# Hash attention and two dense layers: weight loads six slots later, a move two slots later, warm products without a buffer, PSUM halves exchanged

## The chip, the cores and the metric

One core of one Trainium2 chip. The metric is the device time of one execution in microseconds. TensorE (PE) multiplies matrices into PSUM, which has eight banks; VectorE (DVE), ScalarE (ACT) and GpSimd (POOL) do the rest; SyncE (SP) issues nearly all DMAs. Each engine works through its own instructions in order, so an instruction that waits holds up all that stand behind it on its engine. That holds for SP as well: a DMA whose wait is not over keeps the later DMAs from being issued.

## The reference

Attention over 2 batches, 8 heads, 768 positions of width 64, then two dense layers on 1536 tokens of width 512 with an inner width of 2048.

```
q_bits = (q @ proj > 0);  k_bits = (k @ proj > 0)      # 6 bits each
mask   = bucket(q_bits)[:, None] == bucket(k_bits)[None, :]
scores = where(mask, q @ k.T / sqrt(64), -1e9)
attn   = exp(scores - max) / (sum + 1e-9)
x      = attn @ v, heads side by side                  # 1536 x 512
h = x @ w_in;  g = h * tanh(softplus(h));  x = g @ w_out
h = x @ w_in2; g = P(h) / (Q(h) + 1e-6);   out = g @ w_out2
```

P is a cubic and Q a quadratic in h. The weights come as 64-bit numbers and are turned into fp32 pairs (a rounded high part and the rest), and every large product is done as three products of such parts.

## The kernel before, in words

**Attention.** The 16 heads run one behind the other in a software pipeline of *slots*, six to a head: slot 6h + c computes the scores of chunk c of head h (`st`) and, for the head after it, the products from which the row maxima come (`smax`). A table `order` gives every step its first slot, and within a slot the steps go out in the table's order. In the last slot of a head come the value products (`pv`, L307, 24 matmuls), the sums (`dsum`, L431), and for every second head `vsum`. So the PE alternates: six score slots, then a value block.

**What a head needs beforehand.** Head h needs in SBUF: `qB` (rounded q, with the codes of q in rows 0 to 31 and the negated row maxima in row 31), `qX` (the rest of q, in whose first 64 rows a copy of the rounded half belongs) and `KK`. The maxima of head h come from `smax(h, 0..5)`, are gathered on VectorE by `fin_a` (tile `stt`) in slot 6h - 1, and `fin_b` writes them into row 31 of `qB` with four small DMAs, two issued by SP and two by GpSimd. The first score product of head h (L406) waits for these. `move_k` and `move_x` copy parts of k into `KK`; `move_h(h)` (L265) copies 64 rows of `qB` into `qX`, over rows that `move_x(h)` (L261) reads.

**Buffers w0, w1, w2.** The raw input of head h (`load`, L219, slot 6h - 24) lies in buffer w0, w1 or w2, by h modulo 3. Its last readers are `lo(h)` on VectorE (L70, tile qX) and `codes(h)` on the PE, in slot 6h - 7. After the last heads the three buffers take weight chunks 0, 1 and 2 of the first dense layer: `first(f, n)` (L552) loads quarter n of chunk f from a scratch copy in DRAM, in slots FIRST[f] + 2n, from SP. With the values before, chunk 1 starts in slot 66, chunk 2 in slot 72 and chunk 0 in slot 78. The last users of the buffers are head 13 (w1, slot 71), head 14 (w2, slot 77) and head 15 (w0, slot 83).

**Ring.** `weights` converts weight chunks beside the heads: every six slots one ring load (L119), three VectorE operations (L100 to L106), a split on GpSimd, and for chunks 0 to 2 two stores to the scratch copy (L138, L139).

**After a head.** `evac` and `devac` (ScalarE, L447 and L456) read the value block's PSUM tile; `gather`, `recip`, `store` and `spread` bring the reciprocal sums back through SP's DMAs.

**PSUM.** In attention all tiles come from a pool of four buffers of two banks each (`two_banks`). In the opening, `warm(n)` issues n small products of ones whose result nobody reads; they had a tile of their own. After attention the dense stage opens two pools of four banks: `hp` for the first product of a layer (L686), `yp` for the second (L704, L706). The pool that is opened first gets the lower four banks. A dense tile waits for the readers of the attention tile that held its banks.

**Dense stage.** Step i multiplies chunk f of block t (12 matmuls into an h tile), ScalarE and VectorE turn it into g (L729, L730, L70), and 12 matmuls add into four y tiles. Beside the first steps VectorE converts the remaining weight chunks.

Of the kernel before, what the change touches and what calls it, by code (L numbers as in the profile page):

```python
# [9 lines left out]
F32 = mybir.dt.float32  # L10
# [6 lines left out]
PSUM = bass.MemoryType.PSUM  # L17
# [8 lines left out]
NC = S // 128  # L26
BIG = 2.0 ** 40
NBITS = 6
EARLY, SHARED, FIRST = 7, 3, (78, 66, 72, 60, 60, 60, 60)
W_AT, W_LEAD = 5, 4  # L30
POOL_LO = (("lo", 1), ("lo", 2))
ENG = dict(
    lo="dd", hi="aa", xhi="a", xlo="dd", whi="pppp", wlo="pppp",
# [11 lines left out]
def attention_moe_moe(ctx: ExitStack, tc: tile.TileContext, kq, v, proj2, cst, eye, w1, w2, ab, out):  # L45
    nc = tc.nc

    def pool(stack, name, bufs=1, **kw):
        return stack.enter_context(tc.tile_pool(name=name, bufs=bufs, **kw))
# [120 lines left out]
    def attention(actx, tctx):  # L170
# [9 lines left out]
        ring[0] = pool(actx, "ring0", RING[0])  # L180
        ps = pool(actx, "ps", 4, space=PSUM)

        def two_banks(name):
            return ps.tile([128, 2, 512], F32, tag="s", name=name)

        p_raw = ac.tile([128, 64], F32, tag="pr", name="pr")
        cs_t = ac.tile([32, 4], F32, tag="cst", name="cst")
# [8 lines left out]
        ones = v_p.tile([128, 32], F32, tag="ones", name="ones")  # L196
        wones = v_p.tile([128, 128], F32, tag="wones", name="wones")
# [126 lines left out]
        def codes(h):  # L324
            if not 0 <= h < B * H:
                return
            p = [two_banks("cp") for _ in range(1 + (h == 0))]
            ct[h] = p[0][:, 0], p[-1][:, 1]
            code_products(h)


        warm_up = []

        def warm(n):
            if not warm_up:
                warm_up.append(two_banks("wm")[:, 0])
            for _ in range(n):
                nc.tensor.matmul(out=warm_up[0][0:32, 0:128], lhsT=ones, rhs=wones, start=True, stop=True)  # L338

        def code_k(h, of=(0, 1)):  # L340
            if not 0 <= h < B * H:
# [24 lines left out]
        def smax(h, c):  # L366
            if not 0 <= h < B * H:
                return
            if c == 0:
                mt[h] = sm_p.tile([128, NC], F32, tag="m", name="m")  # L370
            p = two_banks("mp")
            for a in range(2):
                nc.tensor.matmul(  # L373
                    out=p[:, a, 0:HALF], lhsT=qB[h % 4][:, c * 128:(c + 1) * 128], rhs=qhalf(KK[h % 4][:, 0], a),
                    start=True, stop=True,
                )
            nc.vector.tensor_reduce(out=mt[h][:, c:c + 1], in_=halves(p), op=ALU.max, axis=AX.XY)  # L377
# [167 lines left out]
        def first(f, n):  # L545
# [26 lines left out]
            ("lo", lo, -7, 1),  # L572
            ("code_q", code_q, -7, 1),
            ("move_x", move_x, -7, 1),
            ("move_h", move_h, -7, 1),
            ("recip", recip, 11, 1),
            ("store", store, 11, 1),
            ("norm", norm, 23, 0),
# [6 lines left out]
            ("gather", gather, 6, 1),  # L585
            ("spread", spread, 12, 1),
            ("vred", vred, -6, 0),
            ("load", load, -24, 1),
            ("load_v", load_v, -10, 0),
            ("first", first, FIRST, -2),  # L590
# [29 lines left out]
        def coef():  # L620
            nc.scalar.activation(out=babs, in_=ab_t[:, 4:6], func=ACT.Abs)

        start = (
            ("get", 0), ("load", 0), ("get", 1), ("load", 1), ("load", 2), ("warm", 5), ("khi", 0), ("qhi",), ("codes", 0),
            ("khi", 2), ("klo",), ("warm", 4), ("signs", 0), ("qlo",), ("hi", 1), ("khi", 1), ("get", 2), ("move_x", 0),
            ("smax", 0, 0), ("warm", 1), ("move_k", 1), ("lo", 1), ("smax", 0, 1), ("warm", 1), ("hi", 2), ("lo", 2),
            ("move_h", 0), ("load", 3), ("smax", 0, 2), ("warm", 1), ("move_x", 1), ("smax", 0, 3), ("warm", 1),
            ("smax", 0, 4), ("warm", 1), ("smax", 0, 5), ("codes", 1), ("fin_a", 0), ("fin_b", 0), ("code_k", 1),
            ("code_q", 1), ("move_k", 2), ("load_v", 0), ("move_h", 1), ("warm", 4),
            ("warm", 4), ("st", 0, 0), ("smax", 1, 0), ("coef",),  # L630
        )

        def run():
            memsets()
            fns = {o[0]: o[1] for o in order}
            fns.update(get=get, coef=coef, khi=khi, qhi=qhi, qlo=qlo, klo=klo, signs=signs)
            done.update((name, (0,)) for name in ("hi", "lo", "move_k", "code_k", "code_q"))
            for name, *k in start:
                if name == "warm":
                    warm(*k)  # L640
                    continue
                done.add((name, tuple(k)))
                fns[name](*k, **({"fn": lo_pool} if (name, *k) in POOL_LO else {}))
            for g in range(last):
                slot_ops(g)
# [7 lines left out]
    def moe(mctx, tctx, tail):  # L653
        by_tile = dict(reuse_waits="tile")
        w2pool = pool(mctx, "w2", **by_tile)
        ring[1] = pool(mctx, "ring1", RING[1], **by_tile)
        g_p = pool(mctx, "g", GB, **by_tile)
        t_p = pool(mctx, "t", 2, **by_tile)
        hp = pool(mctx, "hp", 4, space=PSUM, **by_tile)
        yp = pool(mctx, "yp", 4, space=PSUM, **by_tile)  # L660
        late = []

        def wp(f):
# [214 lines left out]
    with tc.manual_schedule():  # L878
        nc.scalar.preload_act_table_set("natural_log_exp_and_others")
        tctx = ExitStack()  # L880
        with ExitStack() as actx:
            run, tail = attention(actx, tctx)
            run()
        with ExitStack() as mctx:
            run = moe(mctx, tctx, tail)
            run()
# [55 lines left out]
```

## Time and profile before

| | us |
|---|---|
| median of 3 runs | 787.3 (786.08 to 787.31) |
| the profiled execution | 787.76 |
| its span (first to last instruction) | 786.0 |
| PE busy | 763.2 |
| VectorE busy | 588.0 |
| ScalarE busy | 420.9 |
| GpSimd busy | 73.3 |

Attention ends at about 256 us of the span, the first dense layer at about 520. In the profile a group of instructions is named by its line, engine and tiles (`sp<-qB,kk` is a product of qB and kk into the tile sp). Busy shares come in 40 slices of 19.65 us each; PEclk is the clock granted to the PE, in tenths of full speed. An idle time in brackets is the engine's idle time before the instruction, with what ended it.

### The profile page before, as it was taken

To read this page: it belongs to the slowest core of one execution; us is meant where nothing else is said; L and a number is where in the kernel's file an instruction comes from. 1 tells how busy PE (TensorE), PEld (TensorE's weight loads), DVE (VectorE), ACT (ScalarE), POOL (GpSimd) and SP (SyncE) were. 2 spreads that over 40 slices of the span, in tenths; PEclk is the share of its full clock that TensorE was granted. 3 is DMA by queue.
4 is the path that set the end of the run, shared out by engine and by line. 5 is a ranking of instruction groups with operands and counts; after the bars stand their busy time and mean duration, and the time that the engine had idled before them with its cause. 6 is when DMAs were issued, how large, how long until landed. Compare 5 with 4: busy or idle time off the path is not lost.

```text
span 786.0 us, 11698 instructions
## 1 busy us (share of the span) xinstructions
PE 763.2 (97%) x4172; PEld 600.6 (76%) x4172; DVE 588.0 (75%) x1084; ACT 420.9 (54%) x684; POOL 73.3 (9%) x103
## 2 busy tenths in 40 slices
PE   9999999997789999999999999999999999999998
PEld 4767767675566788888888888887888888888886
DVE  5687888885563689855646677659998988888886
ACT  3556656564345444332121333468886766777764
POOL 6323223331210000000000000000000000000000
PEclk9999999999889999999999999999999999999999
DMA  4765764655541434425544588420000100010001
GB/s 132 186 191 162 221 188 110 189 144 137 145 121 34 150 126 148 148 67 168 172 147 161 168 259 267 159 80 1 1 1 1 54 0 1 1 44 11 1 0 55
DMA packets 56650, 85.50 MB, mean 109 GB/s; under 512 B 20112, under 2 KB 28304, under 8 KB 56592
## 3 DMA queue, kind: packets, MB, share of 16 engines
q1 hardware_dynamic: 55424, 84.69, 36.1%
q8 instruction: 33, 0.54, 0.3%
q14 instruction: 25, 0.20, 0.1%
q0 software_dynamic: 1024, 0.03, 0.1%
q10 hardware_dynamic: 144, 0.03, 0.0%
HBM read 57.71 MB, written 14.73 MB: 92 GB/s over the span
## 4 chain that ended last, share of the span: by engine, by line
PE 88%; DVE 5%; DMA 3%; ACT 2%; SPq 1%; issue 1%; DVEq 0%; ACTq 0%
PE h L686 30%; PE y L706 17%; PE y L704 14%; PE sp L406 9%; PE pv L307 6%; PE mp L373 5%; PE pv L431 3%; DMA qB<-stt 2%; PE cp L319 1%; PE wm L338 1%; DVE w L70 1%; DVE t L103 1%; SPq L552 1%; DVE r L106 1%; DMA r<-w 1%
## 5 line engine op out<-in xcount | busy, mean ns | idle before, releaser
L686 PE MATMUL h<-xh,w 128*128 128x512 f32 x768 | 205.0, 389 | 1.6 <-ACT dv L456 1.6
L686 PEld LDWEIGHTS h<-xh,w 128*128 128x128 f32 x768 | 144.2, 188 | 32.0 <-ACT dv L456 2.0
L377 DVE TENSOR_REDUCE m<-mp 128x1 f32<-128x768 f32 x96 | 91.9, 958 | 39.6 <-PE mp L373 35.1
L70 DVE TENSOR_TENSOR gl<-ep,gh 128x512 fp32r<-128x512 f32 x96 | 65.9, 686 | 71.0 <-ACT ep L730 70.0
L729 ACT ACTIVATE gh<-h 128x512 fp32r<-128x512 f32 x48 | 28.7, 599 | 151.1 <-PE h L686 137.9
L686 PE MATMUL h<-xl,w 128*128 128x512 f32 x384 | 102.6, 389 | 0.0
L706 PE MATMUL y<-w,gh 128*128 128x512 f32 x384 | 96.3, 389 | 0.0
L704 PE MATMUL y<-gh,w 128*128 128x512 f32 x384 | 94.8, 389 | 0.0
L411 ACT ACTIVATE e<-sp 128x768 f32<-128x768 f32 x96 | 76.1, 814 | 26.8 <-PE sp L406 25.1
L706 PEld LDWEIGHTS y<-w,gh 128*128 128x128 f32 x384 | 72.1, 188 | 14.9
L686 PEld LDWEIGHTS h<-xl,w 128*128 128x128 f32 x384 | 72.1, 188 | 15.0
L704 PEld LDWEIGHTS y<-gh,w 128*128 128x128 f32 x384 | 72.1, 188 | 15.0
L406 PE MATMUL sp<-qB,kk 128*128 128x384 f32 x192 | 53.9, 363 | 15.0 <-DMA qB<-stt 14.7
L307 PE MATMUL pv<-e,vf 128*64 128x384 f32 x384 | 64.7, 487 | 0.0
L736 ACT ACTIVATE ep<-h 128x512 f32<-128x512 f32 x48 | 28.6, 595 | 52.1 <-PE h L686 52.1
L106 DVE SCALAR_TENSOR_TENSOR r<-r,t 128x256 int32<-128x256 int32 (+1 forms) x114 | 52.1, 457 | 4.7
L103 DVE SCALAR_TENSOR_TENSOR t<-r,t 128x256 int32<-128x256 int32 (+1 forms) x114 | 52.2, 458 | 3.9
L373 PE MATMUL mp<-kk,qB 128*128 128x384 f32 x192 | 53.9, 364 | 0.0
L706 PE MATMUL y<-w,gl 128*128 128x512 f32 x192 | 53.3, 392 | 0.5 <-DVE gl L70 0.4
L307 PEld LDWEIGHTS pv<-e,vf 128*64 128x64 f32 x384 | 27.4, 137 | 34.1 <-issue 33.8
L738 DVE TENSOR_TENSOR n<-n,ep 128x512 f32<-128x512 f32 x48 | 33.1, 690 | 26.9 <-ACT n L737 26.9
L704 PE MATMUL y<-gl,w 128*128 128x512 f32 x192 | 51.4, 390 | 0.1
(79 smaller groups left out, 1038.3 us busy)
## 6 DMA issues: line engine op xcount, KB each, us to landing
r<-w SPq DMA_DIRECT2D x100, 256.0 KB
w<-r SPq DMA_DIRECT2D x64, 128.0 KB
w<-w SPq DMA_DIRECT2D x16, 512.0 KB
r<-w SPq DMA_DIRECT2D x14, 512.0 KB
kq<-kq SPq DMA_DIRECT2D x16, 384.0 KB
kk<-qB SPq DMA_DIRECT2D x15, 384.0 KB
kk<-qX SPq DMA_DIRECT2D x16, 192.0 KB
qX<-qB SPq DMA_DIRECT2D x16, 192.0 KB
```

The lines of the kernel that those rows point to most:

```text
L70: nc.vector.tensor_tensor(out=o, in0=i, in1=f32(h), op=ALU.subtract)
L103: lambda: nc.vector.scalar_tensor_tensor(out=t, in0=r[:, :, 1], scalar=-0x40000000, in1=t, op0=ALU.bitwise_and, op1=ALU.bitwise_or),
L106: lambda: nc.vector.scalar_tensor_tensor(out=o, in0=r[:, :, 0], scalar=29, in1=t, op0=ALU.logical_shift_right, op1=ALU.bitwise_or),
L307: nc.tensor.matmul(out=o[64 * a:64 * a + 64, 0:HALF], lhsT=w, rhs=qhalf(x, a), start=start, stop=stop)
L373: nc.tensor.matmul(out=p[:, a, 0:HALF], lhsT=qB[h % 4][:, c * 128:(c + 1) * 128], rhs=qhalf(KK[h % 4][:, 0], a), start=True, stop=True,)
L377: nc.vector.tensor_reduce(out=mt[h][:, c:c + 1], in_=halves(p), op=ALU.max, axis=AX.XY)
L406: nc.tensor.matmul(out=p[:, a, 0:HALF], lhsT=kk[:, c * 128:(c + 1) * 128], rhs=qq[:, a * HALF:(a + 1) * HALF], start=(i == 0), stop=(i == 1),)
L411: nc.scalar.activation(out=wide(e), in_=halves(p), func=ACT.Exp, scale=1.0 / D ** 0.5)
L686: nc.tensor.matmul(out=p, lhsT=w[:, c * 128:(c + 1) * 128], rhs=x[:, c, :], start=(n == 0), stop=(n == 11))
L704: nc.tensor.matmul(out=y[m], lhsT=w[:, DM + m * 128:DM + (m + 1) * 128], rhs=g, **s)
L706: nc.tensor.matmul(out=y[m], lhsT=g[:, m * 128:(m + 1) * 128], rhs=w[:, DM:2 * DM], **s)
L738: nc.vector.tensor_tensor(out=v_, in0=v_, in1=u, op=ALU.mult)
```

## The change

`FIRST` moves the loads of chunks 0, 1 and 2 six slots later each (84, 72, 78 in place of 78, 66, 72). `move_h` goes from slot 6h - 7 to slot 6h - 5, and in the table from behind `move_x` to behind `vred`. `warm` takes the tile that the next call of `two_banks` will return and writes into that, where it had one of its own; the single warm products after `smax(0, 0)` and `smax(0, 1)` are gone. `yp` is opened before `hp`.

```diff
-EARLY, SHARED, FIRST = 7, 3, (78, 66, 72, 60, 60, 60, 60)
+EARLY, SHARED, FIRST = 7, 3, (84, 72, 78, 60, 60, 60, 60)
...
+        ahead = []
+
         def two_banks(name):
-            return ps.tile([128, 2, 512], F32, tag="s", name=name)
+            return ahead.pop() if ahead else ps.tile([128, 2, 512], F32, tag="s", name=name)
...
-        warm_up = []
-
         def warm(n):
-            if not warm_up:
-                warm_up.append(two_banks("wm")[:, 0])
+            if not ahead:
+                ahead.append(two_banks("wm"))
             for _ in range(n):
-                nc.tensor.matmul(out=warm_up[0][0:32, 0:128], lhsT=ones, rhs=wones, start=True, stop=True)
+                nc.tensor.matmul(out=ahead[0][0:32, 0, 0:128], lhsT=ones, rhs=wones, start=True, stop=True)
...
             ("move_x", move_x, -7, 1),
-            ("move_h", move_h, -7, 1),
             ("recip", recip, 11, 1),
...
             ("vred", vred, -6, 0),
+            ("move_h", move_h, -5, 1),
             ("load", load, -24, 1),
...
-            ("smax", 0, 0), ("warm", 1), ("move_k", 1), ("lo", 1), ("smax", 0, 1), ("warm", 1), ("hi", 2), ("lo", 2),
+            ("smax", 0, 0), ("move_k", 1), ("lo", 1), ("smax", 0, 1), ("hi", 2), ("lo", 2),
...
+        yp = pool(mctx, "yp", 4, space=PSUM, **by_tile)
         hp = pool(mctx, "hp", 4, space=PSUM, **by_tile)
-        yp = pool(mctx, "yp", 4, space=PSUM, **by_tile)
```

## Rows read from the trace of the kernel before

**Rows 1.** The page: busy share of the PE, and its granted clock in 40 slices.

```profile
PE 763.2 (97%) x4172; PEld 600.6 (76%) x4172; DVE 588.0 (75%) x1084; ACT 420.9 (54%) x684; POOL 73.3 (9%) x103
...
PEclk9999999999889999999999999999999999999999
```

**Rows 2.** The PE's waits: line, what it waited for, us in total, times, longest.

```profile
PE sp L406 <- DMA qB<-stt: 14.7, 3, 5.8
PE h L686 <- ACT dv L456: 1.6, 1, 1.6
```

**Rows 3.** Timeline (start us, us, instruction): value products of heads 9 to 14.

```profile
151.96 4.04 PE L307 MATMUL pv<-e,vf 128*64 128x384 f32 x24
...
165.93 4.04 PE L307 MATMUL pv<-e,vf 128*64 128x384 f32 x24
...
179.47 4.04 PE L307 MATMUL pv<-e,vf 128*64 128x384 f32 x24
...
199.80 4.04 PE L307 MATMUL pv<-e,vf 128*64 128x384 f32 x24
...
220.27 4.04 PE L307 MATMUL pv<-e,vf 128*64 128x384 f32 x24
...
239.32 4.09 PE L307 MATMUL pv<-e,vf 128*64 128x384 f32 x24
```

**Rows 4.** Timeline from 180 to 192 us: the first of the three waits.

```profile
180.08 0.21 DVE L386 STREAM_TRANSPOSE stt<-smt 128x32 f32<-128x32 f32 x1
...
182.45 0.33 SPq L552 DMA_DIRECT2D w<-w  x1
...
184.25 1.49 SPq L392 DMA_DIRECT2D qB<-stt  x2
...
191.23 0.98 PE L406 MATMUL sp<-qB,kk 128*128 128x384 f32 x2 [5.09 <-DMA qB<-stt]
```

**Rows 5.** SP's own waits: us in total, times, longest.

```profile
SPq L265 <- DMA kk<-qX: 51.7, 15, 5.5
...
SPq L552 <- DVE qX L70: 16.7, 3, 6.0
...
SPq L219 <- PE sp L406: 2.0, 6, 0.5
```

**Rows 6.** Chain of waits (start us, us, what): opening, first wait, first products after it.

```profile
8.55 0.56 PE wm L338 x2
9.11 0.94 PE mp L373 x2
...
16.08 1.48 PE cp L319 x4
...
21.69 0.35 PE mp L373 x2
...
27.24 0.80 PE cp L319 x4
...
185.04 6.05 DMA qB<-stt
...
192.85 0.64 PE mp L373 x2
```

**Rows 7.** Windows: from 192 us, busy times, then PEclk, DMA share, GB/s.

```profile
192.00:193.00 1.00, 1.00 (x5) 1.00 (x5) 0.00 (x0) 0.06 (x1) 0.00 (x0) 0.50 0.01 3
```

**Rows 8.** Line L392 (fin_b), its own view: landings of the pieces that GpSimd issues.

```profile
DMA to landing us min/median/max: 1.5/1.9/3.9
```

**Rows 9.** Timeline from 257 to 263 us: the seam to the dense stage.

```profile
257.61 1.20 PE L686 MATMUL h<-xh,w 128*128 128x512 f32 x4 [1.64 <-ACT dv L456]
...
260.74 0.60 ACT L729 ACTIVATE gh<-h 128x512 fp32r<-128x512 f32 x1 [1.88 <-PE h L686]
...
261.86 0.69 DVE L70 TENSOR_TENSOR gl<-ep,gh 128x512 fp32r<-128x512 f32 x1 [9.95 <-ACT ep L730]
```

**Rows 10.** DMA issues by line: the ring's stores of 256 KB.

```profile
w<-r SPq DMA_DIRECT2D x12, 256.0 KB
```

## The prediction

> **What bounds the kernel now.** I read the busy shares first, then the PE's own waits, then the timeline of the places where it waits. The PE is busy 97% of the span and every other engine 75% or less [rows 1], so time is lost only where the PE stands idle or runs slowly. The list of its waits names two that this change can reach: 14.7 us in three waits of the score products (L406) for the DMA that writes the row of maxima into qB, and 1.6 us of the first dense product for the last devac (L456) [rows 2]. In the busy shares the clock line shows 8 instead of 9 in two slices, just where the three waits lie: the PE comes back from them at the lower of its two levels [rows 1].
>
> What one of the three costs is read from the starts of the value products (L307, one group per head). Undisturbed heads start 13.97 and 13.54 us apart in turn (151.96, 165.93, 179.47; the longer one holds the vsum products). Then come 20.33, 20.47 and 19.05 us [rows 3].
>
> Where it comes from: the row of maxima is ready on VectorE at 180.08 + 0.21 = 180.29, but SP issues its half of the row's DMAs (fin_b) only at 184.25. Ahead of it in SP's order stands a load of `first` (L552), which got off at 182.45 [rows 4]. SP's waits give the reason: L552 waited three times, 16.7 us together, for the lo of a head (VectorE qX, L70) [rows 5]. In the code, `first(1, 0)` sits in slot 66 and overwrites the buffer w1, which holds head 13's input; that input is read last by lo(13) and codes(13) in slot 71. So SP stands from slot 66 to slot 71, and fin_b(12) of slot 71 is behind it. The same goes for f = 2 (slot 72, lo(14) in slot 77) and f = 0 (slot 78, lo(15) in slot 83).
>
> **The change part by part.**
>
> *Loads six slots later.* `first(1, 0)` goes to slot 72, `first(2, 0)` to 78, `first(0, 0)` to 84: each one slot after its buffer's last reader. That this distance suffices the kernel already shows: the loads of q and k (L219) stand one slot after the reader of their buffer, and their longest wait is 0.5 us [rows 5]. So SP is free when the maxima are ready, as in heads 0 to 11. What goes: 20.33 - 13.97 = 6.36; 20.47 - 13.54 = 6.93; and 19.05 less an undisturbed 13.97 - 0.80 = 13.17 (this head computes no further codes, whose products take 0.80 [rows 6]) = 5.88. [...]
>
> What is late next? Row ready at 180.29, the PE free at 191.23 - 5.09 = 186.14: 5.85 us of cover. SP's two issues take 1.49 [rows 4], so 4.36 us are left for the landing. The pieces that GpSimd issues landed after 1.9 us in the median and 3.9 at most [rows 8]: that fits. It does not fit if bulk loads are ahead: behind the burst of four to five loads that SP had let go at once, the landing took 6.05 us [rows 6], 1.7 more than the cover. In the new order the loads of slots 72, 74 and 76 have no wait, so SP issues them as soon as it gets there: 1.64 us into the head, when devac is done (as at the seam [rows 9]), and then eight issues (gather, spread, load, ring load, move_h, v, two loads) of 0.33 to 0.75 each (a single one and half of the double one in [rows 4]), so by 4.3 to 7.6 us. The row is ready 13.97 - 5.85 = 8.1 us into the head. Each load is 128 x 512 x 4 bytes, 256 KB; in heads 1 to 6 SP stored two pieces of 256 KB per head [rows 10] and loaded a head's input (128 x 768 x 4 bytes, 384 KB) besides, which these heads no longer do. Three or four loads (768 to 1024 KB) stand in place of 896 KB that those heads carried without a wait of the PE. Bounds 0 to 3 x 1.7 us of new idle; I take 0, nearest to those heads.
>
> [...]
>
> The late users also move: weights 0 are complete after `first(0, 3)`, now in slot 90; before their first product lie the scores of slots 90 to 95 and head 15's value and sum products. Cost 0; without that cover one landing, 1.9 to 6 us [rows 6, 8].
>
> *move_h two slots later.* It copies q's rounded half (192 KB) into qX after move_x has read there. In its old place SP stood 51.7 us in 15 waits of up to 5.5 us for that landing [rows 5]; queued behind it were store, the ring's stores, gather, spread, the input load and the ring load. In the new place move_x has long landed, and these six go out up to 3.4 us (51.7 / 15) earlier, except that gather still waits for devac. The PE waited for none of them, so the gain is 0 at the end. Its price: move_h now goes out behind gather, spread, the input load and the ring load: 1.64 us until devac is done and four issues of at most 0.75 make 4.6 us into a head of 13.5. Its reader is the next head's first score product. Even 5.5 us of flight, the longest wait for such a move, leaves 3.4 us. Bounds 0 to a few us in all; I take 0.
>
> *Unread products in the next tile.* The warm products no longer hold a buffer of their own, and two single ones go, after smax(0, 0) and smax(0, 1). One takes 0.56 us on the PE's chain [rows 6], and up to the first score product nothing else is on that chain. VectorE's reductions run beside it; without that cover they would be the bound and the gain of the second warm would go. Gain 2 x 0.56 = 1.12. Bounds: the turn from a warm to a maxima product also goes; a pair takes 0.64 at the lower level [rows 6] and 0.94 beside a warm, so up to 0.30 more each: 1.72. On the low side, the code products took 1.48 us at 16.08 and 0.80 at 27.24 [rows 6]: the opening runs at the slow pace, though the clock line shows its first slice as 9 [rows 1]. If the change of pace stays where it was in time, the 1.12 us brought forward run slowly and lose 1.12 x (1 - 0.35 / 0.64) = 0.51: 0.61 is the lower bound. I take 1.12.
>
> [...]
>
> *First dense products in the upper banks.* The first dense product waits 1.64 us for the last devac [rows 9]: its tile lies on banks that pv(15) still holds. With yp opened first, the h tiles get the upper four banks. If pv(15) stays in the lower half, the first h tiles lie on score tiles that were read by exp long before, and the 1.64 us go. Next in line is ScalarE's Mish (gh at 260.74): it stood idle 1.88 us until the product group was there, so it can follow by 1.64; and VectorE stood idle 9.95 us before gl, released by ScalarE's ep [rows 9], so its long run of conversions starts earlier by the same. Bounds 0 to 1.64; I take 1.64.
>
> Sum: 19.17 + 0 + 1.12 + 1.64 = 21.93. The profiled execution took 787.76 us, the median of the runs is 787.3: 787.76 - 21.93 - 0.46 = **765.4 us**.
>
> **Rivals.**
>
> 1. *The seam keeps its wait.* Without the warm tile's own buffer the rotation of the four score buffers shifts, and pv(15) may land in the upper half. For it: the wait of [rows 9] depends on nothing but where pv(15) lies. Against it: the order of tiles per head is unchanged, so the buffers should only trade names. 765.4 + 1.6 = 767.0.
>
> 2. *The loads are still ahead of the row.* Same queue, 256 KB pieces two slots apart, the last one in slot 76 before fin_b in slot 77. For it: 6.05 us of landing [rows 6]. Against: SP runs ahead and has issued the last one 0.5 to 3.8 us before the row is ready (8.1 less 7.6 and 4.3). One to three heads late by 1.7 us, with up to 1.5 us of lower clock each ((19.17 - 14.7) / 3): 767 to 775, all three without the clock 770.5.
>
> 3. *The change does not do what it says*: the first load still waits, for the reader one head on, and fin_b of that head stands behind it. Against: the buffers w1, w2, w0 get no input after heads 13, 14 and 15. Only seam and opening gain: 787.3 - 1.64 - 1.12 = 784.5.
>
> 4. *Slower: move_h comes too late.* In its new place it is behind the bulk loads in SP's queue; if it lands after the head's last sums, each of 15 heads begins with a wait. It decides once a head's wait exceeds 21.9 / 15 = 1.5 us, which is a landing 10.4 us after an issue at 4.6. At 2 us a head it is 765.4 + 30 = 795. Against it: no such move took over 5.5 us [rows 5].
>
> **How the numbers follow.** Forecast 0.62 (own range 763.8 to 767), rival 1 0.10, rival 2 0.16, rival 3 0.05, rival 4 0.03, still better than forecast 0.04. The range 763.8 to 770.6 holds forecast, rival 1 and rather over half of rival 2, about 0.82. Two tenths of a per cent, 1.6 us, is what a measurement of this kernel can tell from no change. Faster 0.95: all the cases but rival 4 make 0.97, of which 0.02 go to within 0.2%, for a rival 3 in which the other gains fail too; slower 0.03, rival 4.
>
> **What would show it.** Right: no wait of L406 for qB<-stt; starts of value products 13.5 to 14 us apart up to head 14; no lower clock between 180 and 240 us; SP's L552 without a wait for qX, L265 with next to none for kk; the first dense product directly behind the last sums; the first score product 1.1 us earlier. Wrong: a wait of L406 for qX<-qB (rival 4), landings of qB<-stt over 4.4 us (rival 2), or a wait for dv at L686 (rival 1).

## The result, and the profile after

| | before | after |
|---|---|---|
| median of the runs, us | 787.3 (786.08 to 789.42, 4 runs) | 767.24 (765.59 to 768.86, 4 runs) |
| profiled execution, us | 787.76 | 766.72 |
| its span, us | 786.0 | 764.9 |

The ratio after / before is 0.9742 with a 95% interval of [0.9712, 0.9773]: faster by 20.1 us. The forecast was 765.4, with a range of 763.8 to 770.6.

Two lines of the page after, the PE's busy share and its granted clock, answer to [rows 1]: the two slices at 8 are gone.

```profile
PE 753.5 (99%) x4168; PEld 594.5 (78%) x4168; DVE 587.3 (77%) x1084; ACT 420.5 (55%) x684; POOL 73.4 (10%) x103
...
PEclk9999999999999999999999999999999999999999
```

The PE's waits after (us in total, times, longest) answer to [rows 2]. The 14.7 us of the score products are down to one wait of 2.2, and the dense product's wait for dv is gone. A wait of 2.8 us is new: that of the first score product of all, which the names call wm, since it now uses the tile of the warm products.

```profile
PE wm L406 <- DMA qB<-stt: 2.8, 1, 2.8
PE sp L406 <- DMA qB<-stt: 2.2, 1, 2.2
```

SP's waits after, for [rows 5]: L552 waits for no qX any more, and the move (L267, before L265) waited once instead of 15 times.

```profile
SPq L267 <- DMA kk<-qX: 1.3, 1, 1.3
...
SPq L552 <- PE mp L373: 0.8, 2, 0.5
```

Timeline after, value products of heads 11 to 14, for [rows 3]:

```profile
177.22 4.04 PE L309 MATMUL pv<-e,vf 128*64 128x384 f32 x24
...
191.18 4.04 PE L309 MATMUL pv<-e,vf 128*64 128x384 f32 x24
...
206.61 4.04 PE L309 MATMUL pv<-e,vf 128*64 128x384 f32 x24
...
220.15 4.09 PE L309 MATMUL pv<-e,vf 128*64 128x384 f32 x24
```

The three intervals are 13.96, 15.43 and 13.54 us, where [rows 3] has 20.33, 20.47 and 19.05. The one at 15.43 holds the wait of 2.2. With them the 21.1 us by which the two spans differ can be split, each part from the two timelines:

| part | before | after | gain, us |
|---|---|---|---|
| opening, up to the first value product | 27.86 | 25.81 | 2.05 |
| from there to the value products of head 11 | 151.61 | 151.41 | 0.20 |
| intervals 11 to 12, 12 to 13, 13 to 14 | 59.85 | 42.93 | 16.92 |
| 14 to 15 | 10.47 | 10.47 | 0 |
| last value products to first dense product | 7.82 | 6.11 | 1.71 |
| from there to the end | 528.39 | 528.17 | 0.22 |

### The profile page after: what moved, and what is told of

The parts are those of the page before. It is cut to its first block, busy times and chain, and to the rows that moved or that the text cites. A ratio compares the mean times of both kernels' runs of the same rounds, so it can differ in the third digit from the quotient of the medians.

```text
span 764.9 us, 11693 instructions
## 1 busy us (share of the span) xinstructions
PE 753.5 (99%) x4168; PEld 594.5 (78%) x4168; DVE 587.3 (77%) x1084; ACT 420.5 (55%) x684; POOL 73.4 (10%) x103
## 4 chain that ended last, share of the span: by engine, by line
PE 91%; DVE 4%; DMA 2%; ACT 1%; issue 1%; POOL 0%; SPq 0%; DVEq 0%; POOLq 0%
PE h L686 32%; PE y L704 17%; PE y L706 16%; PE sp L406 9%; PE pv L309 8%; PE pv L431 4%; PE mp L373 4%; PE cp L321 1%; DMA qB<-stt 1%; DVE m L377 1%; DMA r<-w 1%; PE pv L290 1%; ACT e L411 0%; DMA pr<-proj 0%; DVE w L70 0%
## 5 line engine op out<-in xcount | busy, mean ns | idle before, releaser
L377 DVE TENSOR_REDUCE m<-mp 128x1 f32<-128x768 f32 x92 | 88.0, 957 | 31.3 <-PE mp L373 26.9
L411 ACT ACTIVATE e<-sp 128x768 f32<-128x768 f32 x95 | 75.1, 814 | 18.1 <-PE sp L406 16.5
L406 PE MATMUL sp<-qB,kk 128*128 128x384 f32 x190 | 51.6, 353 | 2.5 <-DMA qB<-stt 2.2
L406 PE MATMUL sp<-qX,kk 128*128 128x384 f32 x190 | 49.0, 339 | 0.0
```

Of the source, the lines that this page charges most:

```text
L406: nc.tensor.matmul(out=p[:, a, 0:HALF], lhsT=kk[:, c * 128:(c + 1) * 128], rhs=qq[:, a * HALF:(a + 1) * HALF], start=(i == 0), stop=(i == 1),)
L411: nc.scalar.activation(out=wide(e), in_=halves(p), func=ACT.Exp, scale=1.0 / D ** 0.5)
```

## The experiments

E1 to E4 ran on one chip (the kernel before there: 784.92, 783.42 to 787.26), E5 to E8 on one (before: 786.38, 782.97 to 789.0), E9 and E10 on one (before: 783.9, one run). Times are compared with the kernel before on the same chip.

Three things were to be explained: the wait left in the interval 12 to 13, the wait that went at the seam, and the opening.

**E1, only the loads.** The kernel before with the first edit alone.

```diff
-EARLY, SHARED, FIRST = 7, 3, (78, 66, 72, 60, 60, 60, 60)
+EARLY, SHARED, FIRST = 7, 3, (84, 72, 78, 60, 60, 60, 60)
```

> The kernel before with the three loads six slots later and nothing else. Theory A (bulk transfers ahead of the row of maxima make head 13 late, wherever move_h stands): the three waits of L406 become one of about 2 us, in head 13; the seam keeps its 1.6 us wait for dv; 787.3 - 16.9 = 770.4 us. Theory B (the late row comes from move_h in its new place, 192 KB more in the burst): no wait of L406 at all, 787.3 - 19.2 = 768.1 us.

Measured: 768.43 us (767.56 to 769.99), ratio 0.9789 [0.9759, 0.9819]. Its intervals are 13.98, 13.72 and 14.26: 17.89 us less than in the profile before, by one line. The PE's waits of E1:

```profile
PE sp L406 <- DMA qB<-stt: 3.6, 3, 2.0
PE h L686 <- ACT dv L456: 1.6, 1, 1.6
```

Of the 3.6 us, 2.0 lie in the opening, so the row of maxima was late by 1.6 us in two heads, 1.2 at most. Neither theory is borne out as it stands: the interval 12 to 13 is at 13.72, without theory A's wait of about 2 us, and theory B allowed no wait at all. By the medians on this chip the line is worth 16.5 us, by the ratio's interval 14.2 to 18.9; the 17.89 of the traces lies in that, the forecast 19.17 doesn't. The wait at the seam is still there.

**E2, move_h back in its old place.** The changed kernel without its second edit.

```diff
+            ("move_h", move_h, -7, 1),
...
-            ("move_h", move_h, -5, 1),
```

> The changed kernel with move_h back in its old place. Theory A: head 13 still waits 1.5 to 3 us for its row, SP stands about 50 us for move_x again, and the time is within 0.7 us of the changed kernel's 767.2. Theory B: the wait in head 13 goes, 765.3 us.

Measured: 765.78 (764.53 to 770.02), ratio 0.9763 [0.9726, 0.9799]. The intervals are 14.09, 13.54 and 13.62, sum 41.25 against 42.93: the wait in the interval 12 to 13 is gone, and one of 0.5 us stands in the next. Between these two profiles the new place of move_h costs 1.68 us. The medians don't settle that: the ratios of E2 and of the change overlap. The other profiles with the loads moved agree in direction but not in size: after the opening the PE waits 1.7 to 2.3 us for the row in the five with move_h in its new place (the change, E4, E5, E6, E10), and 1.6, 0.5, 0 and 0 us with it in the old one (E1, E2, E7, E8). Where the cost may come from shows in SP's own line. First the changed kernel's timeline, from 185 us on:

```profile
185.66 0.61 SPq L464 DMA_DIRECT2D cs<-dv  x1
...
186.95 0.54 SPq L552 DMA_DIRECT2D w<-w  x1
...
187.58 0.39 SPq L119 DMA_DIRECT2D r<-w  x1
...
188.06 0.47 SPq L267 DMA_DIRECT2D qX<-qB  x1
...
188.63 0.67 SPq L227 DMA_DIRECT2D vf<-v  x1
...
189.35 1.99 SPq L552 DMA_DIRECT2D w<-w  x2
...
191.79 0.21 DVE L386 STREAM_TRANSPOSE stt<-smt 128x32 f32<-128x32 f32 x1
192.06 1.96 SPq L392 DMA_DIRECT2D qB<-stt  x2
...
199.50 0.58 PE L406 MATMUL sp<-qB,kk 128*128 128x384 f32 x2 [2.20 <-DMA qB<-stt]
```

Then the same stretch of E2:

```profile
183.40 0.47 SPq L267 DMA_DIRECT2D qX<-qB  x1
...
187.37 0.37 SPq L119 DMA_DIRECT2D r<-w  x1
...
187.83 0.68 SPq L227 DMA_DIRECT2D vf<-v  x1
...
188.56 2.22 SPq L552 DMA_DIRECT2D w<-w  x2
...
190.88 0.21 DVE L386 STREAM_TRANSPOSE stt<-smt 128x32 f32<-128x32 f32 x1
```

In E2 the 192 KB of move_h (qX<-qB) are issued at 183.40, before devac's cs<-dv; in the changed kernel they stand at 188.06, between the ring's load and v. Windows of 1 us tell what the DMA engines had to do in between (the last two columns are DMA share and GB/s). The changed kernel:

```profile
185.00:186.00 1.00, 1.00 (x7) 0.74 (x5) 0.90 (x1) 0.99 (x3) 0.74 (x1) 1.00 0.00 0
186.00:187.00 1.00, 1.00 (x7) 0.89 (x6) 0.72 (x2) 1.00 (x2) 0.00 (x0) 1.00 0.02 3
```

E2:

```profile
184.00:185.00 1.00, 0.89 (x6) 0.57 (x5) 0.94 (x1) 0.98 (x3) 1.00 (x1) 1.00 0.47 108
185.00:186.00 1.00, 1.00 (x7) 1.00 (x8) 0.53 (x2) 1.00 (x2) 0.12 (x1) 1.00 0.44 92
```

So in its old place the copy ran in a gap that is empty in the changed kernel (DMA share 0.00 and 0.02), and in the new one it adds to the burst ahead of the row. The changed kernel's chain of waits shows what the row's DMA then takes, from its issue on GpSimd to the landing:

```profile
192.64 0.58 POOL qB L392
193.22 6.08 DMA qB<-stt
```

**E3, only move_h.** The kernel before with the second edit alone (the diff is that of E2, turned round).

> The kernel before with move_h two slots later and nothing else. Theory A: SP's waits for move_x (L265) fall from 52 us to under 3, the PE's waits stay 3 and about 15 us, and the time stays within 0.2% of 787.3. Rival: the ring's loads and the stores that stood behind move_h matter to the three waits, and the time falls or rises by 2 us or more.

Measured: 793.55 (792.37 to 795.0), ratio 1.0108 [1.0082, 1.0134]: 8.6 us slower than before. The intervals are 22.43, 23.39 and 21.20. PE's and SP's waits:

```profile
PE sp L406 <- DMA qB<-stt: 23.0, 5, 7.4
```

```profile
SPq L552 <- DVE qX L70: 25.5, 3, 9.6
```

SP's timeline of E3, where the first blocked load gets off at 181.48:

```profile
181.48 0.33 SPq L552 DMA_DIRECT2D w<-w  x1
181.91 0.38 SPq L119 DMA_DIRECT2D r<-w  x1
182.38 0.48 SPq L265 DMA_DIRECT2D qX<-qB  x1
182.91 1.11 SPq L552 DMA_DIRECT2D w<-w  x2
184.06 1.52 SPq L392 DMA_DIRECT2D qB<-stt  x2
```

Two slots later puts move_h(12) into slot 67, behind the load of slot 66 that blocks SP. It is let go together with three loads and goes out ahead of the row; in the kernel before SP issues the same between 182.45 and 184.25, without the qX. Theory A expected no change. The rival left a rise open, but through the ring's loads and stores, not through move_h itself. So the second edit does harm by itself, and costs little only behind the first.

**E4, hp opened first again.** The changed kernel without its last edit (one run).

```diff
         hp = pool(mctx, "hp", 4, space=PSUM, **by_tile)
+        yp = pool(mctx, "yp", 4, space=PSUM, **by_tile)
```

> The changed kernel with hp opened before yp again. Theory C (taking away the warm products' own buffer alone already moves the last value tile off the first h tile's banks): the first dense product starts right behind the last sums, no wait at L686, 767.2 us. Theory D (the exchange of the halves is what does it): L686 waits 1.6 us for dv, 768.9 us.

Measured: 765.65. The first dense product has no wait: it starts at 235.66, before devac starts at 236.99.

```profile
235.66 1.19 PE L686 MATMUL h<-xh,w 128*128 128x512 f32 x4
...
236.99 0.33 ACT L456 ACTIVATE dv<-pv 128x192 f32<-128x192 f32 x1
```

E1 and E3, which have the loads or the move alone, keep the wait. So the third edit, the warm products without a buffer, takes it away without the exchange; that pv(15) then lies on other banks is read from the missing wait, no trace shows the banks.

**E9, only the exchange of the halves.** The kernel before with yp opened first (one run).

> The kernel before with yp opened before hp and nothing else. Theory C (either of the two edits alone takes the first h tile off the last value tile's banks): no wait of L686 for dv, the first dense product starts right behind the last sums, three waits of L406 as before. Theory D (both are needed): the wait of 1.6 us stays.

Measured: 784.95, and again no wait at the seam:

```profile
255.23 1.19 PE L686 MATMUL h<-xh,w 128*128 128x512 f32 x4
```

Devac here ends at 256.56 + 0.33, after that product began. Either edit alone removes the wait of 1.64 us, and both together no more than one. In the time of these single runs (783.9 before) it doesn't show: E9's three intervals make 61.53 us where those of the profile before make 59.85.

**E10, the two single warm products back.** The changed kernel, and only these two products again (one run).

```diff
-            ("smax", 0, 0), ("move_k", 1), ("lo", 1), ("smax", 0, 1), ("hi", 2), ("lo", 2),
+            ("smax", 0, 0), ("warm", 1), ("move_k", 1), ("lo", 1), ("smax", 0, 1), ("warm", 1), ("hi", 2), ("lo", 2),
```

> The changed kernel with the two single warm products back behind smax(0, 0) and smax(0, 1), written into the next tile. Theory F (with the clock up early, VectorE's reductions set the opening and the two products only delay its second and third reduction): the first score product starts 13.3 to 13.6 us after the first code product, against 12.7 to 13.2 in the five runs with the changed opening; if the clock stays low, 1.1 us later than without them. Theory G (the PE's chain sets it at either clock): 1.1 us later, 13.9 to 14.3.

Measured: 765.59; the first score product starts 13.78 us after the first code product, between what the two theories expect. One run is too few, but every profile holds a sample. With the two products it is 13.34, 13.59, 14.03 and 13.78 (E1, E3, E9, E10; mean 13.69); without them 12.75 to 13.17 in seven (the change, E2, E4 to E8; mean 13.06). So the two are worth about 0.6 us. E10's chain of waits fits that: it holds one of the two (0.57 us from 8.54) and then leaves the PE for VectorE's last five reductions (4.51 us from 9.98), beside which the second runs. The profile before is an outlier by another cause, at 16.51 (the first code product at 4.21):

```profile
20.72 0.61 PE L406 MATMUL sp<-qB,kk 128*128 128x384 f32 x2
```

The changed kernel's chain of waits in the opening shows that cause beside [rows 6]:

```profile
7.61 0.68 PE wm L373 x2
...
8.31 5.29 DVE m L377 x6
...
15.39 1.62 DMA qB<-stt
...
17.11 0.93 PE wm L406 x4
```

In [rows 6] the chain stays on the PE up to the first score product, at 20.72, a warm product (listed as x2) takes 0.56 and four code products still take 1.48 at 16.08. Here it leaves the PE after the first maxima and goes over VectorE's six reductions and the landing. In its timeline a warm product takes 0.41 from 8.92 on, where that of before has 0.64 up to 14.50. By these durations the PE went over to the faster pace some 12 us sooner, and it idled 2.81 us for the row. The windows print a granted clock of 1.00 for both stretches, so what sets the two paces isn't shown.

**E5, the change again**, for the chip of E6 to E8.

> The changed kernel itself, beside the next three on one chip. Theory B (in its old place move_h's copy fills a gap in the DMA traffic at the start of head 12; in the new place it stands among the loads ahead of the row): head 13 waits about 2.2 us again, its value products start 15.4 us after head 12's. The first score product starts at 17.1 to 17.5, or near 19.6 if the opening runs at the lower clock.

Measured: 766.26 (765.15 to 767.01), ratio 0.974 [0.9707, 0.9772]; the interval 12 to 13 is 15.44, with the wait of 2.2 again.

**E6, the loads apart.** The changed kernel, with one load in head 12, four each in heads 13 and 14, and three in head 15.

```diff
+LOADS = {1: (72, 78, 78, 80), 2: (80, 84, 84, 86), 0: (86, 90, 90, 92)}
...
-                todo = [(at[f] + 2 * n, (f, n)) for f in range(EARLY) for n in range(4)]
+                todo = [(LOADS[f][n] if f in LOADS else at[f] + 2 * n, (f, n)) for f in range(EARLY) for n in range(4)]
```

> The changed kernel with 1, 4, 4 and 3 of the twelve 256 KB loads in heads 12 to 15 in place of 3, 4, 4 and 1; move_h in its new place. Theory A and B alike (what counts is how many bytes are on the DMA engines ahead of the row): head 13's wait of 2.2 us goes, head 12 to 13 takes 13.5 us, 1.9 us less than the changed kernel. Rival (the 192 KB copy alone is what makes the row late): the wait stays above 1 us.

Measured: 764.83 (763.68 to 766.75), ratio 0.9718 [0.9678, 0.9758]. The interval 12 to 13 is 13.55, its wait gone; but 2.2 us of waits for the row turned up in two others, 6 to 7 (14.18) and 13 to 14 (14.29). In the interval 6 to 7 there is none of the moved loads, but the late move_h, which every head has; E3 has such a wait of 0.8 us too, between heads 4 and 5.

**E7, E6 with move_h in its old place.**

> As the one before, with move_h back in its old place as well. Theory B: no wait of L406 for the row after the opening; heads 12 to 14 as without loads, and the time 1.7 to 2.2 us under the changed kernel's, the same as the one before within 0.4. Rival (the old place costs something that the new one saves, as SP stands 50 us there): 0.5 us or more above the one before.

Measured: 764.26 (763.58 to 764.95), ratio 0.9716 [0.9683, 0.9748]. No wait for the row is left after the opening; the intervals are 13.97, 13.55 and 13.55. Against E6 the medians don't differ beyond their scatter.

**E8, E7 with 18 instead of 8 warm products ahead of the first score product.**

```diff
-            ("warm", 4), ("st", 0, 0), ("smax", 1, 0), ("coef",),
+            ("warm", 14), ("st", 0, 0), ("smax", 1, 0), ("coef",),
```

> As the one before, with 18 warm products ahead of the first score product in place of 8. Theory E (in the opening VectorE's reductions and the row's landing set the first score product, the PE idles 2 to 2.8 us before it, and in some executions the clock falls after that and costs 1.6 us): no idle before the first score product, no lower clock in the first head, 0 to 1.6 us less. Rival (the ten products are on the chain): the first score product starts 1 us or more later, 1 to 4 us more.

Measured: 763.71 (763.45 to 764.03), ratio 0.9709 [0.9678, 0.974]. It beats both kernels: its slowest run is below the fastest of the change on the same chip (E5, 765.15). Against E7 the ten products alone aren't told apart, since the runs overlap. The waits of the PE in E8 (one line of the code further down):

```profile
PE wm L407 <- DMA qB<-stt: 0.4, 1, 0.4
```

What the ten products bridge is told by windows of the opening, with the PE's busy share first and its clock ahead of the last two columns. The changed kernel, idle from 14.3 to 17.1:

```profile
16.00:17.00 1.00, 0.00 (x0) 0.00 (x0) 0.00 (x0) 0.67 (x2) 0.00 (x0) 1.00 0.03 2
...
19.00:20.00 1.00, 1.00 (x5) 1.00 (x5) 0.55 (x1) 0.13 (x1) 0.00 (x0) 0.50 0.94 213
```

E8:

```profile
16.00:17.00 1.00, 0.88 (x9) 0.60 (x6) 0.00 (x0) 0.88 (x2) 0.14 (x1) 1.00 0.04 3
...
19.00:20.00 1.00, 1.00 (x8) 1.00 (x7) 0.92 (x2) 0.86 (x3) 0.00 (x0) 1.00 1.06 238
```

## Why the prediction was right, step by step

**The loads.** Right in mechanism, with the size off. With the loads behind the last reader SP stands free, and E1 gives 17.89 us for that line alone in the traces. The forecast was 19.17, the sum of its 6.36, 6.93 and 5.88. It put an undisturbed interval 13 to 14 at 13.17, the longer interval less the 0.80 of the codes that this head doesn't compute; without any late row it is 13.54 (E8). The chain of waits of E8 in that interval shows where 0.37 came back:

```profile
209.75 0.55 PE pv L291 x4
...
210.51 0.58 ACT ev L448
...
211.71 0.33 ACT dv L457
212.04 0.71 ACT e L412
...
212.79 0.96 PE sp L407 x4
```

After the vsum products the chain leaves the PE and comes back over ScalarE's two copies and its exp. By E8's timeline the third score product starts 2.64 us after the first, against 2.40 in the interval 11 to 12, where the chain stays on the PE; with the next product behind it that makes 0.28. The codes themselves gave 0.70, not 0.80: the last maxima product and the value products start 0.44 us apart, against 1.14 with the codes. Why the detour over ScalarE comes in this head isn't shown; the interval 12 to 13, which has the codes, has one as well. So 18.8 were to be had, not 19.17, and 16.92 came.

**move_h at 0.** This step failed. The prediction asked when move_h's reader needs it, found 3.4 us to spare, and that was so: no wait for qX<-qB appears. It counted move_h among the eight issues ahead of the row, but not its 192 KB among the bytes ahead of it. E2 against the change puts them at 1.68 us (41.25 and 42.93); over all profiles with the loads moved, the waits for the row average 2.1 us with the new place and 0.5 with the old. The prediction's own lines held the number: issues by 4.3 to 7.6 us into the head, 8.1 until the row. In the changed kernel the head begins at 183.9, as the vsum products end; the last bulk issue ended at 191.34, 7.4 us into it and 0.66 before the row was ready at 191.79 + 0.21 = 192.00. The two issues took 1.99 us, not 2 x 0.75. From 192.00 on the PE had 5.30 us of cover (it was free at 199.50 - 2.20); GpSimd began its second issue 1.22 after the row, the landing took 6.08 from there and the start 0.20 more: 7.50 less 5.30 are the 2.20. That is rival 2, in one head, and by the copy together with the loads. The prediction's sign for that rival came too: a landing of over 4.4 us. In the interval 13 to 14 four loads go out, but without v's load; the last issue ended 2.36 us before the row was ready, and nothing waits.

**Why [rows 5] gave no warning.** The 15 waits of SP for the move, 51.7 us, looked like a cost. E2 and E8 have them too (48.6 and 47.6 us) and are no slower. SP stands there until move_x has landed, and then issues move_h into the gap. The loads behind it wait for devac in any case: the first of them goes out at 186.73 in E2 and at 186.95 in the changed kernel.

**The warm products.** The term was 1.12; the two profiles show 2.05 for the whole opening, and like for like the products are worth about 0.6. The mechanism was right for the profile that was read, in which the PE ran slowly up to about 20 us (sixteen warm products took 3.30 us from 17.49 on, and 1.93 in the changed kernel) and stood on the chain alone. It doesn't hold where the faster pace comes sooner: then VectorE's reductions set the first score product from the second warm product on, the case that the prediction named as the cover that would go. That 2.05 came out is luck of the two executions: it holds a late shift of pace before and, after, a stretch at a granted clock of 0.50 (the first value products at 25.81, against 24.41 in E2). The prediction's lower bound was 0.61, for a shift of pace that stays where it was in time. The size comes out so, but not by that path: E10 has the two products and had gone over to the faster pace as early (a warm product takes 0.41 from 9.87 us on), so no run here tells whether the two products move that shift.

**The seam.** 1.64 forecast, 1.71 measured. The prediction gave it to the exchange of the halves and feared the tile without a buffer (rival 1). E4 and E9 show that each alone does it; neither harms the other.

**The sum** came within 1.84 us. The terms make 0.83 of that: 21.93 forecast, 21.10 in the two profiles, as 16.92 for 19.17, 2.05 for 1.12, 1.71 for 1.64 and 0.42 scattered over the rest; by luck the opening, which gave more than its term, hid part of what the loads and move_h gave less. The other 1.0 is that the profiled execution of the changed kernel lies 0.52 under its median, and that of before 0.46 above. The measured 767.24 lies just above the forecast's own range (763.8 to 767), where rival 2 begins. Rival 3 is excluded by SP's waits, rival 4 by the PE's.

## What to carry to other kernels

A DMA of 0.8 KB on the critical chain can pay for the bytes issued ahead of it (here 6.1 us to land, where 1.5 is the least), not only for the waits ahead of it; when loads are moved, list what lands between them and the row, and look for stretches with a DMA share near 0 (here 0.00 and 0.02) to put copies in. An edit that costs 1 to 2 us behind another may cost 8.6 without it, so undo each alone before its price is called nothing. A step of a chain that was read from one profile holds at the pace of that profile (here 0.64 or 0.41 us for a warm product, listed as x2): see whether another one runs it at the other pace.

## What the runs showed of the hardware that was not expected

The PE goes over to the faster pace at different times in executions of the same opening instructions. By the warm products (timeline: 0.64 us for one at the slow pace, 0.41 at the fast one) it did so 8 to 10 us into the span in E1, E3 and E9, and at about 20 us in the profile before, which open as they do. An idle stretch of 1.9 to 2.8 us ahead of the first score product was followed by a granted clock of 0.50 for some 3 us in five of the profiles (the change, E1, E3, E5, E6) and by no fall in E2, E4, E7, E9 and E10. Among those without the two single products the first value products start at 25.55 to 25.97 us with it and at 24.41 to 24.57 without. E8, which closes the stretch to 0.4, had runs within 0.6 us of each other; those of E7, which is E8 without the ten products, spread over 1.4 us, and those of the change over 1.9 and 3.3. That the idle causes the fall isn't shown: half of the profiles with it have none.

Pieces issued by GpSimd landed late behind SP's bulk loads too: 6.08 us above, after the two loads that SP issued from 189.35 to 191.34. The view of L392 in the changed kernel, against the 1.5/1.9/3.9 of [rows 8]:

```profile
DMA to landing us min/median/max: 1.5/2.7/6.5
```

And SP's issue itself took longer in the burst: two loads of 256 KB took 1.99 and 2.22 us above, where the pair in E3, close behind the first load let go, took 1.11. That busy DMA engines are the reason isn't shown: the two issues of the row right behind the slow pair took 1.96 us in the changed kernel, but 1.52 in E2.
